# Linear attention and an MLP on one core: three feature buffers, two x buffers, another order of the first loads, longer runs of half-array matmuls, and a last tile in two column parts

## The chip, the cores and the metric

The kernel runs on one core of a Trainium2 chip. The metric is the time on the device in microseconds. A program written with the Tile framework issues to five engines, each with its own queue: PE (TensorE, matmuls), DVE (VectorE), ACT (ScalarE), POOL (GpSimd) and SP (SyncE, which here only issues DMAs). Each queue runs in order; semaphores order the queues among each other.

## The reference

Eight batches, eight heads, 576 tokens, a head width of 64, 128 features. All inputs are float32, the output too.

```python
def phi(x):
    proj = einsum('bhsd,df->bhsf', x, w_phi)
    proj = proj - max(abs(proj), axis=-1, keepdims=True)
    return concatenate([exp(proj), exp(-proj)], axis=-1)
q_p, k_p = phi(q), phi(k)
kv = einsum('bhsf,bhsd->bhfd', k_p, v)
z = sum(k_p, axis=2)
num = einsum('bhsf,bhfd->bhsd', q_p, kv)
den = einsum('bhsf,bhf->bhs', q_p, z)[..., None] + 1e-06
x = (num / den) laid out as [batch, token, head * 64]          # 8 x 576 x 512
xn = (x - mean(x)) / sqrt(var(x) + 1e-06) * g_ln               # over the 512 columns
out = x + maximum(xn @ w_ch1, 0) @ w_ch2                       # 512 -> 2048 -> 512
```

## The kernel before, in words

The work is cut into four pairs of batches. A pair has 2 x 576 = 1152 tokens, which are nine tiles of 128 tokens. Tiles 0 to 7 are the first 512 tokens of the two batches; tile 8 holds the last 64 tokens of both (the "tails", tensors kx, qx, vx).

The attention of a pair is done in eight units; there are 32 units in all, numbered 0 to 31. In pairs 1 to 3 a unit is one head of both batches; in pair 0 it is two heads of one batch. Two units form a group, and a load brings k, q or v of a group (of a unit at the very start). A unit runs through these steps:

- q and k are turned so that the head's 64 columns lie on the partitions (tile qkT). In pair 0 TensorE does it (qkT_ps, line 531, with a copy on VectorE or ScalarE); in later pairs an engine casts to bfloat16 (qkb) and a DMA transposes (line 514).
- pm (line 561): the projections of k and of q, eight matmuls each. They use 64 rows of the array, the half `e` for one of two heads or batches. In the profile they are 64*128, all other matmuls 128*128. One side takes two PSUM banks.
- maxima of |pm| on VectorE (line 581); exp of the maxima (emk, emq, line 597) and exp(pm), exp(-pm) of k (EB, line 612) on ScalarE; GpSimd scales v by the maxima (vv, lines 626 to 635).
- pt and ea (lines 656, 662): the features of q in the other layout. The tails have steps of their own: kx and qx transposed (line 400), px (line 410), their maxima mx (line 424), and the exponentials EBx and eax. emk of a group holds the tails' value in one column, written first.
- kv (lines 681, 686) from EB and vv, copied to KV on ScalarE (line 693); num (line 715) from KV and ea, then numc and rden on VectorE (lines 721 to 733) and the division, which writes x on GpSimd (line 739).

EB, vv and ea have two buffers each, x (nine tiles of a pair) has three, and num is cut into parts so that a PSUM bank is enough.

The MLP of a pair takes three tiles at a time. VectorE makes the mean and variance (line 858), VectorE or GpSimd the centred value times g_ln (xc, lines 866 to 876; this is where the norm vector `gln` is read), transposes give xT (TensorE in pair 0, line 923; DMA later, line 908). hT_ps (line 973, function `first`) is a block of 128 of the 2048 hidden columns for 384 tokens, four matmuls of 384 columns; ScalarE or VectorE applies relu into hT (lines 981, 983; 32 buffers). ch_ps (line 1005, function `second`) sums 16 matmuls of 512 columns for one tile; VectorE adds x (the result, line 1012), and SP issues the store (line 951, or line 956 for tile 8, two DMAs). The MLP of a pair is mixed with the attention of the next.

The order of the work is not the order of the loops. Each step is given to a planner (class `Order`) with an estimated duration, the engines that may take it, the keys that it reads and writes, and the resource that it takes (`"B"`: 8 PSUM banks). `due` walks backwards to give each step a rank; `run` then walks forwards, lets each engine take the waiting step of lowest rank whose resources are free, and writes the instructions out in that order. Keys such as `("EA", e, n % 2)` stand for buffers. So a changed number of buffers, load order or rule in `run` gives each queue a new order. The planner's estimates are no measurements.

SP and ACT issue DMAs that share eight semaphores in turn, so a ninth issue waits until the first has landed.

Of the kernel before, what the change touches and what calls it, by code (L numbers as in the profile page):

```python
# [23 lines left out]
LAG = {"PE": 0.24, "DVE": 0.20, "ACT": 0.23, "POOL": 0.22, "SP": 0.1, "DMA": 1.8, "CAST": 1.8}  # L24

# [8 lines left out]
class Order:  # L34
# [73 lines left out]
    def run(self):  # L108
# [13 lines left out]
        while events:  # L122
            now = events[0][0]
            while events and events[0][0] <= now + 1e-9:
                _, kind, _, op, _ = heapq.heappop(events)
                if kind == 1:
                    for engine in op.alts:
                        key = op.ready if engine in ("DMA", "CAST") else op.rank
                        heapq.heappush(waiting[engine], (key, op.number, op))
                elif kind == 0:  # L130
                    for name, n in op.release or ():
                        room[name] += n
            for engine, queue in waiting.items():
                if free[engine] > now + 1e-9 or not queue:
                    continue
                passed, held, op = [], set(), None
                while queue:
                    item = heapq.heappop(queue)
                    op = item[2]
                    if op.taken:  # L140
                        op = None
                        continue
                    if op.acquire is None or (
                        op.acquire[0] not in held and room[op.acquire[0]] >= op.acquire[1]
                    ):
                        break
                    held.add(op.acquire[0])
                    passed.append(item)
                    op = None
                for item in passed:  # L150
                    heapq.heappush(queue, item)
                if op is None:
                    continue
                op.taken, op.at = True, (now, engine)
                if op.acquire:
                    room[op.acquire[0]] -= op.acquire[1]
                us = op.alts[engine]
                if engine == "DMA" and free.get("CAST", 0.0) > now:
                    shared = free["CAST"] - now
                    us = 4.0 * us if 4.0 * us <= shared else us + shared * 0.75  # L160
                end = now + us
                if engine == "PE" and op.rows != rows:
                    rows = op.rows
                    end += 0.1
                lag = LAG[engine] if op.lag is None else op.lag
                free[engine] = end
                done.append((op, engine))
                heapq.heappush(events, (end, 2, op.number, op, None))
                heapq.heappush(events, (end + lag, 0, op.number, op, None))
                for o in op.users:  # L170
                    same = len(o.alts) == 1 and engine in o.alts
                    o.ready = max(o.ready, end + (0.1 if same else lag))
                    o.left -= 1
                    if not o.left:
                        offer(o)
# [8 lines left out]
def kernel(  # L184
# [21 lines left out]
    NT = 9  # L206
# [6 lines left out]
    NBUF = 3  # L213
    RN = 384
# [5 lines left out]
    NX = 3  # L220
# [21 lines left out]
    ea_bufs = [consts.tile([P, 2, MX * P], BF16, name=f"ea{i}") for i in range(2)]  # L242
# [5 lines left out]
    sched = Order({"B": 8})  # L248
# [37 lines left out]
    def dma(queue, rank, nbytes, dst, src, r=(), w=()):  # L286
# [7 lines left out]
        add(queue, {"SP": 0.55, "ACT": 0.55, "POOL": 0.84}[queue], rank, emit, r=r, w=(key, *w, *chain), lag=0.0)  # L294
        if queue == "POOL":
            add("CAST", 4.2, rank, None, r=(key,), w=w)
        else:
            add("DMA", nbytes / 340.0 / 1000.0, rank, None, r=(key,), w=w)
# [29 lines left out]
    def load_tails(t, pair, batches, queue, rank):  # L328
        key = "kqv"[0 if t is k else 1 if t is q else 2] + "x"
        for half in range(2):  # L330
            ps_ = slice(half * 64, half * 64 + 64)
            if pair == 0 and t is not q:
                (b,) = batches
                slots = range(4 * b, 4 * b + 4)
                off, step = (b * H + half) * S * D, 2 * S * D
            else:
                slots = range(H)
                off, step = (2 * pair + half) * H * S * D, S * D
            sl = slice(slots[0], slots[-1] + 1)
            if t is v:  # L340
                dst = vx_bufs[pair % 2][ps_, sl, half, 0:D]
            else:
                dst = (qx_bufs if t is q else kx_bufs)[pair % 2][ps_, sl, :]
            dma(
                queue, rank, 25000 * len(slots), dst,
                dram(t, off + 512 * D, [[D, 64], [step, len(slots)], [1, D]]),
                w=[(key, half, pair % 2, s) for s in slots],
            )
# [155 lines left out]
    def a_trans(u, V):  # L504
        n, g = u["n"], u["g"]
        pool, tag, res = ps_B, "B", "B"
        if u["pair"]:
# [14 lines left out]
            add("SP", 1.27, V, turn, r=[("qkb", n % 2)], w=[("turn", n), *ks], lag=0.0)  # L522
            add("DMA", 1.0, V, None, r=[("turn", n), ("qkb", n % 2)], w=ks)
# [28 lines left out]
    def a_main(u, V, sides):  # L552
# [14 lines left out]
        for i in sides:  # L567
# [3 lines left out]
                + ([("EB", e, n % 2) for e in range(2)] if i else []),  # L571
# [3 lines left out]
    def a_side(u, i, V):  # L575
# [32 lines left out]
        def exps(e):  # L608
            if "EB" not in u:
                u["EB"] = att.tile([P, 2, MX, F], BF16, tag="EB", name="EB")  # L610
# [10 lines left out]
        def scale_main(t):  # L621
            if t == 1:
                u["vv"] = att.tile([P, 2, NT + 1, D1], BF16, tag="vv", name="vv")
# [17 lines left out]
        for e in range(2):  # L641
            add("ACT", 0.96, V, lambda e=e: exps(e), r=[("pm", 1, n, e), ("m", 1, n % 3, e)],
                w=[("EB", e, n % 2)], release=[("B", 1)])
        vdata = [*main_keys(u, "v"), *tail_keys(u["pair"], u["slot"], "v")]
        add("POOL", 1.5, V, lambda: scale_main(1), r=[("em", 1, n % 3), *vdata],
            w=[("vv", 1, n % 2)])
        add("POOL", 1.5, V, lambda: scale_main(0),
            r=[("en", n % 3), ("vv", 1, n % 2), *vdata], w=[("vv", 0, n % 2)])

    def a_feat(u, V):  # L650
        n = u["n"]

        def products(e):
            u["EA"] = ea_bufs[n % 2]
# [12 lines left out]
        for e in range(2):  # L667
            add("PE", mm(1, 512), V, lambda e=e: products(e), r=["wb", ("qkT", 0, n % NQ)],
                w=[("pt", n, e), ("EA", e, n % 2)], acquire=("B", 1))
            add("ACT", 0.96, V, lambda e=e: exps(e), r=[("pt", n, e)], w=[("EA", e, n % 2)],  # L670
                release=[("B", 1)])

    def a_kv(u, V):
# [17 lines left out]
        def copy():  # L691
# [5 lines left out]
            r=[(what, t, n % 2) for what in ("EB", "vv") for t in range(2)] + [("EBx", g % 2)],  # L697
# [84 lines left out]
    def nums(u, part, V):  # L782
        n, pair = u["n"], u["pair"]
        x = x_bufs[pair % NX]
        keys = [("EA", 0, n % 2), ("EA", 1, n % 2), ("KV", n % NKV)]
# [61 lines left out]
    def x_stats(pr, r, V):  # L847
# [38 lines left out]
        def rstd():  # L886
            sl = slice(ts[0], ts[-1] + 1)
# [7 lines left out]
    def x_trans(pr, r, slot_c, V):  # L895
# [5 lines left out]
        if pr["pair"]:  # L901
            for i in range(n):
# [10 lines left out]
                add("SP", 1.27, V, turn, r=[("xc", slot_c, i)], w=[key, *wk], lag=0.0)  # L913
                add("DMA", 0.5, V, None, r=[key, ("xc", slot_c, i)], w=wk)
# [32 lines left out]
    def store(pr, t, o):  # L947
        b0 = 2 * pr["pair"]
        if t < MX:
            b, j = b0 + t // 4, t % 4  # L950
            nc.sync.dma_start(
                out=dram(out, (b * S + j) * DM, [[4 * DM, P], [1, DM]]), in_=o
# [7 lines left out]
    HB = 2 * JC  # L960

    def moe(pr, V):
# [34 lines left out]
        def second(r, i0, n, V):  # L997
# [3 lines left out]
            def products():  # L1001
                if j0 == 0:
                    ch[t] = ps_B.tile([P, DM], FP32, tag="B", name="ch_ps")
                for jj in range(j0, j0 + n):
                    nc.tensor.matmul(  # L1005
                        ch[t], hT[r, jj][:, rt * P : (rt + 1) * P], w2_sb[:, jj, :],
# [3 lines left out]
            def result():  # L1010
                ch["o", t] = o = out_pool.tile([P, DM], FP32, tag="o", name="o")
                nc.vector.scalar_tensor_tensor(  # L1012
                    out=o, in0=ch[t], scalar=pr["rstd"][:, t : t + 1], in1=x[:, t, :],
                    op0=ALU.mult, op1=ALU.add,
# [3 lines left out]
            add("PE", mm(n, DM), V, products,  # L1018
                r=[("rstd", pair % 2, t)] + [hkey[r, jj] for jj in js]
                + [("w2", jj) for jj in (js if j0 or pair else range(JC))],  # L1020
                w=[("ch", pair, t)], acquire=("B", 1) if j0 == 0 else None)
            if j0 + n == JC:
                ok = ("o", counts["o"] % 3)
                counts["o"] += 1
                add("DVE", 0.67, V - 30.0, result,
                    r=[("ch", pair, t), ("rstd", pair % 2, t)] + [("x", pair % NX, t, h) for h in range(H)], w=[ok], release=[("B", 1)])
                key = ("store", pair, t)
                add("SP", 0.42 if t < MX else 1.2, 0.0, lambda: store(pr, t, ch["o", t]),
                    r=[ok], w=[key], lag=0.0)
                add("DMA", 0.8, 0.0, None, r=[key, ok])  # L1030

        NR = len(tiles)
        for r in range(NR + 1):
# [5 lines left out]
            for jj in range(JC):  # L1039
# [5 lines left out]
                if r > 0:  # L1045
                    i, end = jj * m, (jj + 1) * m
                    while i < end:
                        n = min(end - i, JC - i % JC)
                        ahead[0] = E_S0 if pair == 0 and r <= TILES0 else E_MOE
                        second(r - 1, i, n, V)  # L1050
                        i += n
                    V += MOE_STEP * m / 3
        return V
# [5 lines left out]
    for p_ in range(NPAIR):  # L1059
        sizes = (3, 3, 3) if p_ == 0 else (3, 3, 3)  # L1060
# [4 lines left out]
        })  # L1065
    for n in range(NU):
# [15 lines left out]
    for half in range(2):  # L1082
        dma("ACT", 0.0, 32768, wphi_f[half * D : (half + 1) * D, :], w_phi, w=[("wphi", half)])
    load_main(q, 0, [0], "ACT", 0.1)
    load_tails(k, 0, [0], "SP", 0.2)
    load_main(v, 0, [0], "SP", 0.3)
    load_tails(v, 0, [0], "SP", 0.4)
    dma("ACT", 0.5, 262144, gln_sb, dram(moe_g_ln, 0, [[0, P], [1, DM]]), w=["gln"])
    load_main(k, 0, [1], "SP", 0.6)
    load_main(q, 0, [1], "ACT", 0.6)  # L1090
# [24 lines left out]

    load_main(k, 2, [0, 1], "SP", 3.0)
# [8 lines left out]
    for n in range(NU + 2):  # L1125
        V = start(n)
        step = start(n + 1) - V
        if n < NU:
# [20 lines left out]
            if n == GATE:  # L1149
                kx1 = kx_bufs[1]  # L1150
                add("POOL", 0.1, V, lambda: nc.gpsimd.memset(kx1[:, :, 0:1], 0.0),
                    r=[("vv", 0, n % 2)], w=[k_ for s_ in range(H) for k_ in tail_keys(1, s_, "k")])
            for i_ in WEIGHTS.get(n, ()):
                after = [("vv", 0, n % 2)]
# [87 lines left out]
```

## Time and profile before

The median of 13 runs is 382.99 us (380.49 to 384.79).

| what | value |
|---|---|
| the profiled execution's own time | 383.77 us |
| its span | 382.0 us |
| mean granted TensorE clock | 0.986 |
| first hT_ps matmul | 46.56 us |
| PE idle, 0 to 20 us | 8.4 us |
| PE idle, 20 to 60 us | 7.6 us |
| PE idle, 60 to 120 us | 3.4 us |
| PE idle, 120 to 300 us | 1.4 us |
| unit 1's first pm matmul | 12.06 us |
| GpSimd's first vv | 10.19 us |
| largest groups on PE: hT_ps, ch_ps | 150.4 us and 148.4 us busy |

A page lists busy time by engine, then 40 slices of the span in which each digit is a busy share in tenths, then DMA queues, the chain of work that ended last, and the costliest groups of instructions. A row of the timeline has the start, the time that the merged instructions cover, engine, line, operation, what is written and read, and a count; in square brackets stand the idle time ahead of it and what ended it. PE matmuls are pipelined: each is shown with its latency, so rows of PE overlap, and the distance of two starts is what a matmul costs.

### The profile page before, as it was taken

To read this page: it belongs to the slowest core of one execution; us is meant where nothing else is said; L and a number is where in the kernel's file an instruction comes from. 1 tells how busy PE (TensorE), PEld (TensorE's weight loads), DVE (VectorE), ACT (ScalarE), POOL (GpSimd) and SP (SyncE) were. 2 spreads that over 40 slices of the span, in tenths; PEclk is the share of its full clock that TensorE was granted. 3 is DMA by queue.
4 is the path that set the end of the run, shared out by engine and by line. 5 is a ranking of instruction groups with operands and counts; after the bars stand their busy time and mean duration, and the time that the engine had idled before them with its cause. 6 is when DMAs were issued, how large, how long until landed. Compare 5 with 4: busy or idle time off the path is not lost.

```text
span 382.0 us, 9102 instructions
## 1 busy us (share of the span) xinstructions
PE 356.2 (93%) x3332; PEld 208.7 (55%) x3332; DVE 280.1 (73%) x722; ACT 251.0 (66%) x641; POOL 205.3 (54%) x365
## 2 busy tenths in 40 slices
PE   4787889899999999998999999999999999999994
PEld 1565656546555555654566545655556546555541
DVE  4799998998989979976779889978688785000111
ACT  3899697698959627876789647866688416433310
POOL 4699687646886728944557467944447432000000
PEclk9989799999999999999999999999999999999999
DMA  7999999955968845384739835612200136110112
GB/s 202 332 274 186 177 314 261 223 126 137 255 148 212 213 144 112 71 231 84 221 76 219 205 99 123 154 30 63 78 0 29 43 96 102 30 52 27 55 41 71
DMA packets 88605, 52.70 MB, mean 138 GB/s; under 512 B 55024, under 2 KB 83824, under 8 KB 88560
## 3 DMA queue, kind: packets, MB, share of 16 engines
q1 hardware_dynamic: 83488, 47.07, 48.2%
q0 software_dynamic: 4224, 4.19, 6.9%
q10 hardware_dynamic: 848, 0.85, 0.8%
q8 instruction: 26, 0.43, 0.5%
q14 instruction: 19, 0.16, 0.2%
HBM read 37.03 MB, written 9.44 MB: 122 GB/s over the span
## 4 chain that ended last, share of the span: by engine, by line
PE 74%; DMA 7%; ACT 7%; DVE 5%; POOL 2%; issue 2%; SPq 1%; DVEq 0%; ACTq 0%; POOLq 0%
PE ch_ps L1005 29%; PE hT_ps L973 28%; PE num L715 4%; DMA qkT<-qkb 4%; PE pm L561 4%; PE kv L686 3%; PE pt L656 3%; ACT EB L612 3%; ACT ea L662 2%; DVE m L581 1%; DMA kx<-in_k_dram 1%; DMA qk<-in_k_dram 1%; PE kv L681 1%; DMA qk<-in_q_dram 1%; POOL vv L626 1%
## 5 line engine op out<-in xcount | busy, mean ns | idle before, releaser
L973 PE MATMUL hT_ps<-xT,w 128*128 128x384 bf16 x768 | 150.4, 326 | 1.4 <-ACT ea L662 0.6
L1005 PE MATMUL ch_ps<-w,hT 128*128 128x512 bf16 x576 | 148.4, 379 | 0.6 <-DVE numc L721 0.6
L983 ACT ACTIVATE hT<-hT_ps 128x384 bf16<-128x384 f32 x127 | 61.8, 496 | 64.4 <-PE hT_ps L973 63.8
L973 PEld LDWEIGHTS <-w 128*128 128x128 bf16 x768 | 71.0, 98 | 53.4 <-issue 2.2
L581 DVE TENSOR_REDUCE m<-pm 128x4 f32<-128x512 f32 x128 | 81.2, 677 | 7.4 <-PE pm L561 7.1
L739 POOL TENSOR_TENSOR x<-numc,rden 128x192 bf16<-128x192 f32 (+1 forms) x112 | 51.6, 471 | 59.7 <-DVE rden L733 59.4
L1005 PEld LDWEIGHTS <-hT 128*128 128x128 bf16 x576 | 52.8, 98 | 48.1 <-issue 0.8
L612 ACT ACTIVATE EB<-pm 128x512 bf16<-128x512 f32 x128 | 69.4, 621 | 8.3 <-DVE m L581 8.1
L662 ACT ACTIVATE ea<-pt 128x512 bf16<-128x512 f32 x128 | 67.2, 627 | 6.1 <-PE pt L656 5.8
L1012 DVE SCALAR_TENSOR_TENSOR o<-ch_ps,rstd,x 128x512 f32<-128x512 f32 x36 | 26.5, 742 | 52.8 <-PE ch_ps L1005 41.0
L626 POOL TENSOR_TENSOR vv<-v,emk 128x512 bf16<-128x512 f32 x32 | 33.5, 1048 | 38.8 <-ACT emk L597 26.3
L721 DVE TENSOR_TENSOR numc<-num,emq 128x195 f32<-128x195 f32 (+1 forms) x96 | 32.2, 346 | 14.4 <-PE num L715 11.7
L981 DVE TENSOR_SCALAR hT<-hT_ps 128x384 bf16<-128x384 f32 x65 | 34.5, 539 | 5.6 <-PE hT_ps L973 5.0
L715 PEld LDWEIGHTS <-ea 128*128 128x128 bf16 x512 | 28.6, 100 | 17.0 <-issue 5.1
L715 PE MATMUL num<-KV,ea 128*128 128x65 bf16 x512 | 31.5, 196 | 3.3 <-ACT KV L693 1.6
L626 POOL TENSOR_TENSOR vv<-v,en 128x512 bf16<-128x512 f32 x32 | 34.4, 1075 | 0.0
L727 DVE TENSOR_TENSOR numc<-numc,num 128x195 f32<-128x195 f32 (+1 forms) x100 | 33.3, 343 | 1.0
L561 PEld LDWEIGHTS <-qkT 64*128 64x128 bf16 x512 | 16.1, 98 | 17.4 <-issue 13.4
L858 DVE BATCH_NORM_STATS2 st<-x 128x6 f32<-128x512 bf16 x36 | 24.2, 672 | 1.2 <-POOL x L739 1.2
L686 PE MATMUL kv<-vv,EB 128*128 128x65 bf16 x512 | 24.9, 198 | 0.0
L686 PEld LDWEIGHTS <-EB 128*128 128x128 bf16 x512 | 22.4, 101 | 2.7 <-issue 0.9
L656 PE MATMUL pt<-qkT,wbk 128*128 128x512 bf16 x64 | 23.3, 410 | 0.1
(67 smaller groups left out, 389.5 us busy)
## 6 DMA issues: line engine op xcount, KB each, us to landing
out_dram<-o SPq DMA_DIRECT2D x32, 256.0 KB, 2.5
qk<-in_k_dram SPq DMA_DIRECT2D x28, 256.0 KB, 4.8
v<-in_v_dram SPq DMA_DIRECT2D x28, 256.0 KB, 3.3
qk<-in_q_dram SPq DMA_DIRECT2D x26, 256.0 KB, 5.3
w<-in_moe_w_ch_dram POOLq DMA_DIRECT2D x8, 512.0 KB, 8.6
qk<-in_k_dram SPq DMA_DIRECT2D x2, 512.0 KB, 6.2
qk<-in_q_dram SPq DMA_DIRECT2D x2, 512.0 KB, 6.9
v<-in_v_dram SPq DMA_DIRECT2D x2, 512.0 KB, 7.1
```

Of the source, the lines that this page charges most:

```text
L581: nc.vector.reduce_max(out=u["m", i].rearrange("p (c e) -> p e c", e=2)[:, e], in_=u["pm", i, e], axis=AX.X, apply_absolute_value=True,)
L612: nc.scalar.activation(u["EB"][:, t, e * 4 : (e + 1) * 4].rearrange("p c f -> p (c f)"), u["pm", 1, e].rearrange("p c f -> p (c f)"), AF.E ...
L626: nc.gpsimd.tensor_tensor(out=u["vv"][:, t, 0:MX, 0:D], in0=vb[:, uu, :].rearrange("p (c d) -> p c d", d=D), in1=bcast(e[:, 0:MX], 2, D), ...
L656: nc.tensor.matmul(u["pt", e], wbk[:, e, :], u["qkT"][:, 0:512], start=True, stop=True)
L662: nc.scalar.activation(u["EA"][:, t, e * 512 : (e + 1) * 512], u["pt", e], AF.Exp, scale=(1.0, -1.0)[t],)
L686: nc.tensor.matmul(ps[:, t, c // 4, :], EB[:, t, (c % 2) * 4 + c // 2, :], vv[:, t, c, :], start=False, stop=(t == 0 and c == MX - 1), ski ...
L715: nc.tensor.matmul(ps[:, t, i, :], lhsT, rhs, start=(j == 0), stop=(j == len(terms) - 1))
L739: nc.gpsimd.tensor_tensor(out=dst, in0=st["numc"][:, i : i + cnt, 0:D], in1=bcast(st["rden"][:, i : i + cnt], 2, D), op=ALU.mult,)
L973: nc.tensor.matmul(st["ps"][:, 0:cols], w1_sb[:, kc, jj * P : (jj + 1) * P], pr["xT", r][:, kc, 0:cols], start=(kc == 0), stop=(kc == KC - 1),
L981: nc.vector.tensor_relu(h_sb[:, 0:cols], st["ps"][:, 0:cols])
L983: nc.scalar.activation(h_sb[:, 0:cols], st["ps"][:, 0:cols], AF.Relu)
L1005: nc.tensor.matmul(ch[t], hT[r, jj][:, rt * P : (rt + 1) * P], w2_sb[:, jj, :], start=(jj == 0), stop=(jj == JC - 1),)
```

## The change

- Buffers: ea, EB and vv have three (`NE`), x has two (`NX`), hT has 28 (`HB`).
- `run`: after a half-array step (`rows`, the pm products) PE takes another such step that is ready, if its PSUM banks are free and its rank is less than `STAY` = 10 behind the first in the queue.
- A resource `"S"` of eight stands for the DMA semaphores in the plan: each SP and ACT issue takes one, its transfer gives it back.
- The first loads: one half of w_phi is issued by SP, k and q of unit 1 come ahead of v of unit 0 and of the tails, and the norm vector is loaded by SP after the groups of units 2 and 3 instead of by ACT among the first.
- The last pair's last three tiles are taken in the order 8, 6, 7; tile 7 is finished in two column parts, 384 and 128 wide, each with its own PSUM tile, result and store. The last step of the loop is emitted after the loop, four matmuls at a time.
- `load_tails` is written differently, with the same loads.

```diff
+STAY = 10.0
...
-                while queue:
+                if engine == "PE" and rows:
+                    near = sorted(i for i in queue if i[2].rows and not i[2].taken)
+                    near = [i for i in near if room[i[2].acquire[0]] >= i[2].acquire[1]]
+                    if near and near[0][0] < queue[0][0] + STAY:
+                        op = near[0][2]
+                while queue and op is None:
...
+    NE = 3
...
-    NX = 3
+    NX = 2
...
-    ea_bufs = [consts.tile([P, 2, MX * P], BF16, name=f"ea{i}") for i in range(2)]
+    ea_bufs = [consts.tile([P, 2, MX * P], BF16, name=f"ea{i}") for i in range(NE)]
...
-    sched = Order({"B": 8})
+    sched = Order({"B": 8, "S": 8})
...
-        add(queue, {"SP": 0.55, "ACT": 0.55, "POOL": 0.84}[queue], rank, emit, r=r, w=(key, *w, *chain), lag=0.0)
+        add(queue, {"SP": 0.55, "ACT": 0.55, "POOL": 0.84}[queue], rank, emit, r=r, w=(key, *w, *chain), lag=0.0,
+            acquire=None if queue == "POOL" else ("S", 1))
...
-            add("DMA", nbytes / 340.0 / 1000.0, rank, None, r=(key,), w=w)
+            add("DMA", nbytes / 340.0 / 1000.0, rank, None, r=(key,), w=w, release=[("S", 1)])
...
-                u["EB"] = att.tile([P, 2, MX, F], BF16, tag="EB", name="EB")
+                u["EB"] = att.tile([P, 2, MX, F], BF16, tag="EB", name="EB", bufs=NE)
...
-                u["vv"] = att.tile([P, 2, NT + 1, D1], BF16, tag="vv", name="vv")
+                u["vv"] = att.tile([P, 2, NT + 1, D1], BF16, tag="vv", name="vv", bufs=NE)
...
-    HB = 2 * JC
+    HB = 28
...
-        def second(r, i0, n, V):
+        def second(r, i0, n, V, c0=0, c1=DM):
...
-                        ch[t], hT[r, jj][:, rt * P : (rt + 1) * P], w2_sb[:, jj, :],
+                        ch[t, c0], hT[r, jj][:, rt * P : (rt + 1) * P], w2_sb[:, jj, c0:c1],
...
+        LAST = (len(tiles[-1]) - 1) * JC
...
+                        if pair == NPAIR - 1 and r == NR and i >= LAST:
+                            break
                         second(r - 1, i, n, V)
...
+        if pair == NPAIR - 1:
+            for c0, c1 in ((0, 384), (384, DM)):
+                for jj in range(0, JC, 4):
+                    second(NR - 1, LAST + jj, 4, V, c0, c1)
+                    V += 1.0
...
+    pairs[-1]["tiles"][-1] = [MX, MX - 2, MX - 1]
...
     load_main(k, 0, [0], "SP", 0.0)
-    for half in range(2):
-        dma("ACT", 0.0, 32768, wphi_f[half * D : (half + 1) * D, :], w_phi, w=[("wphi", half)])
+    for e_, queue in enumerate(("ACT", "SP")):
+        dma(queue, 0.0, 32768, wphi_f[e_ * D : (e_ + 1) * D, :], w_phi, w=[("wphi", e_)])
     load_main(q, 0, [0], "ACT", 0.1)
-    load_tails(k, 0, [0], "SP", 0.2)
+    load_main(k, 0, [1], "SP", 0.2)
+    load_main(q, 0, [1], "ACT", 0.2)
     load_main(v, 0, [0], "SP", 0.3)
-    load_tails(v, 0, [0], "SP", 0.4)
-    dma("ACT", 0.5, 262144, gln_sb, dram(moe_g_ln, 0, [[0, P], [1, DM]]), w=["gln"])
-    load_main(k, 0, [1], "SP", 0.6)
-    load_main(q, 0, [1], "ACT", 0.6)
+    load_tails(k, 0, [0], "SP", 0.4)
+    load_tails(v, 0, [0], "SP", 0.5)
     load_main(v, 0, [1], "SP", 0.7)
...
+    dma("SP", 3.0, 262144, gln_sb, dram(moe_g_ln, 0, [[0, P], [1, DM]]), w=["gln"])
     load_main(k, 2, [0, 1], "SP", 3.0)
```

## The prediction

> **What bounds the kernel now.** I read the page's totals first, then its forty slices, then stages of the span, and last the instructions around one suspected cost.
>
> ```profile
> PE 356.2 (93%) x3332; PEld 208.7 (55%) x3332; DVE 280.1 (73%) x722; ACT 251.0 (66%) x641; POOL 205.3 (54%) x365
> ...
> PE   4787889899999999998999999999999999999994
> ```
>
> TensorE is busy almost everywhere except in the first six slices and the last. The view by stage says how much is left to win (columns: stretch, length, busy time of PE, PEld, DVE, ACT, POOL with counts, clock, DMA share, GB/s):
>
> ```profile
> 20.00:46.50 26.50, 20.69 (x290) 15.31 (x289) 25.81 (x79) 23.21 (x64) 23.82 (x50) 0.82 1.07 207
> ...
> 60.00:120.00 60.00, 56.63 (x609) 33.76 (x605) 54.03 (x142) 48.00 (x128) 41.81 (x74) 1.00 0.81 186
> 120.00:300.00 180.00, 178.58 (x1745) 104.49 (x1744) 150.05 (x382) 128.17 (x327) 108.85 (x182) 1.00 0.48 123
> ```
>
> From 120 us on PE is idle for 1.4 us in 180; nothing there gets shorter unless PE itself does less. From 20 us to 46.5 us (the first hT_ps group starts at 46.56) VectorE is busy for 25.8 of 26.5 us, and ScalarE and GpSimd nearly as long: that stage is limited by the three elementwise engines, and it begins when their first inputs arrive. So the change can gain in three places: an earlier start, less PE work, a shorter end.
>
> **Part 1, fewer changes between half-array and full-array matmuls.** The pm products use 64 rows of the array (64*128), everything else 128. Around one pm block the timeline of PE reads:
>
> ```profile
> 192.97 0.81 PE L973 MATMUL hT_ps<-xT,w 128*128 128x384 bf16 x4
> 193.72 0.40 PE L561 MATMUL pm<-wbk,qkT 64*128 64x128 bf16 x8
> 194.05 0.82 PE L1005 MATMUL ch_ps<-w,hT 128*128 128x512 bf16 x3
> ```
>
> Groups of four hT_ps matmuls that follow each other start 0.65 us apart, so pm could start at 192.97 + 0.65 = 193.62; it starts at 193.72, 0.10 late. It then holds PE for 0.33 us. Where two blocks stand together, the second adds 0.23 only:
>
> ```profile
> 184.90 0.40 PE L561 MATMUL pm<-wbk,qkT 64*128 64x128 bf16 x8
> 185.13 0.39 PE L561 MATMUL pm<-wbq,qkT 64*128 64x128 bf16 x8
> 185.45 0.82 PE L1005 MATMUL ch_ps<-w,hT 128*128 128x512 bf16 x3
> ```
>
> So leaving costs 0.33 - 0.23 = 0.10 us too: 0.10 per change of mode. PE shows no idle time for it; it hides in "busy". I counted the changes in the order written out for each kernel: 106 before, 76 after. Ahead of the first hT_ps they rise from 26 to 30, where PE waits for others anyway. Behind it they fall from 80 to 46: 34 x 0.10 = 3.4 us; I take **-3.2 us**, since PE was busy for only 11.7 of the 13.5 us from 46.5 to 60. The Trainium skill ("TensorEngine Tiling (Array Packing)", Key Properties) says a change of mode drains the array, without a price; "TensorE: Matmul & The Clock Gate" (Single matmul latency) puts the constant part of a lone warm matmul at 166 ns. Priced as a whole lone latency, the estimate would be 34 x 0.166 = 5.6 us. The trace has the thing itself at 0.10, so 3.2 stands and 5.6 is the far end. The near end is 2.2: the same 34 with a third of it spent waiting for other engines.
>
> The price of staying: a pm pair takes two PSUM banks of the eight earlier than before, k and q together four. They come free after four maxima (0.68 us each) on VectorE and four exponentials (0.62) on ScalarE, about 2.7 us. Other groups then have four banks, and one hT_ps group of four and three ch_ps matmuls, which open about one new bank, pass per 1.3 us. In the pair at 184.90 above nothing waited. I cost it at 0; without that cover it is the rival below.
>
> **Part 2, the first loads.** The DMA queue of SP before:
>
> ```profile
> 0.74 0.45 SPq L291 DMA_DIRECT2D qk<-in_k_dram  x1
> 1.25 1.41 SPq L291 DMA_DIRECT2D kx<-in_k_dram  x2
> 2.70 0.72 SPq L291 DMA_DIRECT2D v<-in_v_dram  x1
> 3.56 1.26 SPq L291 DMA_DIRECT2D vx<-in_v_dram  x2
> 6.49 0.37 SPq L291 DMA_DIRECT2D qk<-in_k_dram  x1
> ```
>
> The k of unit 1 is issued at 6.49 only, held by the kx transfer, and on PE the consequence is
>
> ```profile
> 6.61 0.37 PE L400 MATMUL xT_ps<-ident,kx 128*128 128x128 bf16 x2 [1.10 <-DMA kx<-in_k_dram]
> ...
> 10.51 1.03 PE L531 MATMUL qkT_ps<-ident,qk 128*128 128x128 bf16 x8 [0.93 <-DMA qk<-in_k_dram]
> 12.06 0.61 PE L561 MATMUL pm<-wbk,qkT 64*128 64x128 bf16 x8 [0.52 <-DVE qkT L282]
> ```
>
> After, SP issues k0, one half of w_phi, k1, v0, kx (two), vx (two), v1. Five issues of some 0.5 us put k1 at about 1.8 us. kx loses: its second half is queued behind a wait for k0 (landed at 3.52), so it is issued until about 4.3. From issue to landing kx took 3.9 us here, and the 64 KB loads of k tails have a median of 5.7: it lands at **8.2 to 10.0** against 6.5. The skill speaks against the reordering ("DMA: Bandwidth & Descriptors", Issuing engines are not separate DMA queues): all queues share the same 16 DMA engines, so an earlier k1 and v0 are paid for by kx. By that rule alone 2 x 256 KB at the 225 GB/s of the slice from 4 to 8 us put kx at 6.5 + 2.3 = 8.8, within my bracket; the DMA share there is 0.85, so the rule counts.
>
> What waits for kx: in the new PE order the kx transposes stand behind unit 0's pt and ahead of unit 1's pm. Unit 0's pm itself no longer waits for kx: limited by ScalarE's copies of qkT (5.55 + 2 x 0.58), it starts near 6.5 instead of 6.92. Unit 1's pm starts about 1.0 us behind kx's landing (transpose, copy, px), at 9.2 to 11.0 instead of 12.06: 1.1 to 2.9 us earlier. GpSimd gets its first emk later: behind px stand about 3.2 us of ScalarE work (two EB, two ea, two EBx), so vv starts at 12 to 14 instead of 10.19. Against that, GpSimd stood idle for 1.9 us before unit 1's vv (15.10) and 1.5 us at 19.67, idle times that disappear when both units are ready together, as the three vv buffers allow. So GpSimd lies between 1.6 us ahead and 0.2 us behind at 20 us; VectorE, idle for 2.7 us between 8 and 24 us, gains up to 3. I take **-2.0 us** at the first hT_ps, with bounds of +1.5 (kx past its bracket, GpSimd late) and -4 (all of VectorE's idle time, and some of the 3.4 us that PE idles from 60 to 120). The half of w_phi leaves ScalarE's queue (0.5 us, while it waits for TensorE).
>
> The norm vector's load (256 KB) moves from ScalarE's queue to SP's, behind unit 2's and 3's loads and ahead of unit 4's: one issue of 0.5 us and 1 us of transfer, which delay loads that are used 10 us later. Its first reader, xc, runs at 38.98. Cost 0.
>
> **Part 3, buffers.** Three ea, EB and vv decouple the engines; with VectorE busy for 25.8 of 26.5 us that adds nothing beyond part 2. x falls from three buffers to two, so unit 16's and unit 24's first x waits for the last result of pair 0 and pair 1. In the new order 16 hT_ps, 8 pm and 18 kv matmuls, some 3.6 us, lie between pair 1's last ch_ps and that point, against a result of 0.74 us; pair 0 has 8.6 us. Cost 0; without that cover, at most 1 us each. hT falls from 32 to 28 buffers: the 13th hT of a group reuses the first of the group before, read a step (1.3 us) earlier. Cost 0.
>
> **Part 4, the end.** Before:
>
> ```profile
> 376.32 1.41 DVE L1012 SCALAR_TENSOR_TENSOR o<-ch_ps,rstd,x 128x512 f32<-128x512 f32 x2 [5.06 <-PE ch_ps L1005]
> 377.76 1.11 SPq L956 DMA_DIRECT2D out_dram<-o  x2
> ```
>
> PE ends at 376.93, the result at 377.73 (+0.80), the last store is issued at 378.3 (+1.37). After, a full tile's result starts half a microsecond before PE's end (the last eight matmuls are 128 wide, 8 x 0.055); it ends at +0.35, the narrow result (130 columns on VectorE took 0.28) at +0.65. One full and one narrow store issue of 0.36 put the last issue at +0.73: 0.6 us earlier. Sixteen matmuls of 512 columns become 16 of 384 and 16 of 128: at 0.162 + 0.055 against 0.216 almost nothing, at most 0.1. **-0.5 us**, bounds 0 and -1.2.
>
> **Sum.** -3.2 - 2.0 + 0 - 0.5 = -5.7. The profiled execution took 383.77 (span 382.0), so it would take 378.1; the median, 382.99, is 0.8 below it, which gives **377.3**.
>
> **Rivals.** (a) The early start is lost: kx at 10 us or later makes GpSimd late by what the others gain. ScalarE, VectorE and GpSimd, full together from 20 us, speak for it, GpSimd's idle 3.4 us against it. Then 383.0 - 3.2 - 0.5 = 379.3. (b) More is gained: the stalls up to 120 us go too, and the start brings 4: 375.0. (c) Slower: staying in the half-array mode takes PSUM banks before their turn, and PE waits for a free bank once in each of the 24 units of pairs 1 to 3. The wait decides from 5.7 / 24 = 0.24 us a unit; at 0.36, half of one maximum, it costs 8.6, which ends at 386. Against it: pm pairs already stand together without an idle gap. (d) The change does nothing measurable: the stays cost about what they save (0.24 us a unit), 383.
>
> **How the numbers follow.** The forecast 0.52, (a) 0.20, (b) 0.08, (c) 0.14, (d) 0.06. A measurement of this kernel tells about 0.5% (1.9 us) from no change. Faster: 0.52 + 0.20 + 0.08, less 0.02 for the edge of (a): 0.78; same 0.07; slower 0.15. The forecast's own range is 375.5 to 379.2. To leave out 2 in 10, mostly (c), the range runs from 373.5 (switches at 166 ns, start at -4) to 383.5.
>
> **What would show it.** Part 1: fewer entries of pm blocks, pm in runs of 16, PE's idle time from 120 to 300 us still under 3 us; (c) would put new PE waits there, released by VectorE or ScalarE. Part 2: unit 1's pm at 9 to 11 us, vv's first start at 12 to 14, the first hT_ps near 44.5. Part 4: from PE's end to the span's end 4.5 us instead of 5.1. The prediction is wrong if the first hT_ps comes no earlier, or if PE waits grow behind 60 us.

## The result and the profile after

The changed kernel takes 378.96 us (median of 11 runs, 376.92 to 381.53) against 383.19 us for the kernel before (48 runs). The ratio is 0.9897, with a 95% interval from 0.9867 to 0.9927: faster by 1.0%, about 4 us. Ratios leave out executions that took over 1.5% longer than the fastest of the same kernel. The forecast was 377.3 and rival (a) 379.3; the direction and the range were right, and of the 5.7 us expected some 4 came.

The page of the profiled execution (378.96 us, span 377.2 us), first the totals, then PE's forty slices:

```profile
PE 351.7 (93%) x3348; PEld 208.7 (55%) x3348; DVE 280.1 (74%) x726; ACT 251.0 (67%) x638; POOL 208.4 (55%) x367
...
PE   3877699799999999999999999999999999999995
```

PE is busy for 4.5 us less with 16 matmuls more, and the first to fifth and the eighth slice still aren't full. The view by stage of the changed kernel, with the columns that the prediction explained:

```profile
20.00:46.50 26.50, 17.98 (x291) 13.87 (x288) 25.69 (x80) 24.03 (x68) 24.91 (x49) 0.91 1.03 210
46.50:60.00 13.50, 12.83 (x153) 8.45 (x152) 13.04 (x40) 12.37 (x34) 12.78 (x28) 0.92 1.09 249
60.00:120.00 60.00, 57.05 (x621) 34.70 (x618) 56.17 (x144) 48.79 (x129) 43.41 (x77) 1.00 1.08 219
120.00:300.00 180.00, 178.56 (x1759) 105.76 (x1758) 150.25 (x391) 128.41 (x325) 106.95 (x180) 1.00 0.46 116
```

The stage up to 46.5 us is as full on VectorE, ScalarE and GpSimd as before, and it did not become shorter. The first hT_ps matmul, on PE's timeline:

```profile
47.44 1.46 PE L985 MATMUL hT_ps<-xT,w 128*128 128x384 bf16 x4
```

It was at 46.56. From there to PE's last matmul the kernel before needed 376.93 - 46.56 = 330.4 us, the changed one 372.91 - 47.44 = 325.5. PE's idle time explains 1.5 us of these 4.9: from 46.5 to 60 us it fell from 1.76 to 0.67, from 60 to 120 us from 3.37 to 2.95, and behind 120 us it is 1.42 and 1.44. The other 3.4 is work that PE does in less time: 34 changes of mode at 0.10, if the price in the prediction holds. A higher granted clock is not behind it: from 46.5 to 60 us the changed kernel had 0.92 and the kernel before 0.98, from 60 to 300 us both had 1.00. So the two profiled spans differ by +0.9 (start) - 1.5 (waits) - 3.4 (modes) - 0.8 (end) = -4.8 us. This is bookkeeping over one execution of each kernel; the medians and the ratio say 4.2 and 4.0.

### The profile page after: what moved, and what is told of

Read it like the earlier page. It is cut to its first block, busy times and chain, and to the rows that moved or that the text cites. A ratio compares the mean times of both kernels' runs of the same rounds, so it can differ in the third digit from the quotient of the medians.

```text
span 377.2 us, 9121 instructions
## 1 busy us (share of the span) xinstructions
PE 351.7 (93%) x3348; PEld 208.7 (55%) x3348; DVE 280.1 (74%) x726; ACT 251.0 (67%) x638; POOL 208.4 (55%) x367
## 4 chain that ended last, share of the span: by engine, by line
PE 74%; ACT 8%; DMA 8%; DVE 6%; issue 1%; POOL 1%; SPq 0%; DVEq 0%; POOLq 0%
PE hT_ps L985 29%; PE ch_ps L1017 28%; DMA qkT<-qkb 6%; PE num L726 4%; PE pm L572 3%; PE kv L697 3%; ACT EB L623 3%; ACT ea L673 3%; PE pt L667 3%; DVE m L592 1%; DMA qk<-in_q_dram 1%; DMA qk<-in_k_dram 1%; DVE xc L877 1%; PE kv L692 1%; PE px L420 1%
## 5 line engine op out<-in xcount | busy, mean ns | idle before, releaser
L1017 PE MATMUL ch_ps<-w,hT 128*128 128x512 bf16 (+2 forms) x592 | 148.1, 373 | 0.2 <-DVE mv L870 0.2
L592 DVE TENSOR_REDUCE m<-pm 128x4 f32<-128x512 f32 x128 | 80.2, 676 | 8.1 <-PE pm L572 7.9
L1017 PEld LDWEIGHTS <-hT 128*128 128x128 bf16 x592 | 53.8, 98 | 47.6 <-issue 1.2
L750 POOL TENSOR_TENSOR x<-numc,rden 128x192 bf16<-128x192 f32 (+1 forms) x112 | 51.8, 476 | 46.0 <-DVE rden L744 44.5
L623 ACT ACTIVATE EB<-pm 128x512 bf16<-128x512 f32 x128 | 70.3, 636 | 9.0 <-DVE m L592 8.8
L673 ACT ACTIVATE ea<-pt 128x512 bf16<-128x512 f32 x128 | 68.3, 647 | 2.8 <-PE pt L667 2.7
L1025 DVE SCALAR_TENSOR_TENSOR o<-ch_ps,rstd,x 128x512 f32<-128x512 f32 (+2 forms) x37 | 26.7, 729 | 52.7 <-PE ch_ps L1017 40.7
L993 DVE TENSOR_SCALAR hT<-hT_ps 128x384 bf16<-128x384 f32 x66 | 35.6, 547 | 6.4 <-PE hT_ps L985 5.8
L883 POOL TENSOR_TENSOR xd<-x,mv 128x512 f32<-128x512 bf16 x17 | 18.3, 1079 | 14.7 <-DVE mv L870 12.9
L697 PE MATMUL kv<-vv,EB 128*128 128x65 bf16 x512 | 24.0, 196 | 0.0
```

Of the source, the lines that this page charges most:

```text
L592: nc.vector.reduce_max(out=u["m", i].rearrange("p (c e) -> p e c", e=2)[:, e], in_=u["pm", i, e], axis=AX.X, apply_absolute_value=True,)
L623: nc.scalar.activation(u["EB"][:, t, e * 4 : (e + 1) * 4].rearrange("p c f -> p (c f)"), u["pm", 1, e].rearrange("p c f -> p (c f)"), AF.E ...
L673: nc.scalar.activation(u["EA"][:, t, e * 512 : (e + 1) * 512], u["pt", e], AF.Exp, scale=(1.0, -1.0)[t],)
L697: nc.tensor.matmul(ps[:, t, c // 4, :], EB[:, t, (c % 2) * 4 + c // 2, :], vv[:, t, c, :], start=False, stop=(t == 0 and c == MX - 1), ski ...
L750: nc.gpsimd.tensor_tensor(out=dst, in0=st["numc"][:, i : i + cnt, 0:D], in1=bcast(st["rden"][:, i : i + cnt], 2, D), op=ALU.mult,)
L993: nc.vector.tensor_relu(h_sb[:, 0:cols], st["ps"][:, 0:cols])
```

## What happened in the first 20 us

SP's queue, then PE's, in the changed kernel (timeline):

```profile
1.88 0.58 SPq L300 DMA_DIRECT2D qk<-in_k_dram  x1
...
3.01 1.33 SPq L300 DMA_DIRECT2D kx<-in_k_dram  x2
```
```profile
6.02 0.61 PE L542 MATMUL qkT_ps<-ident,qk 128*128 128x128 bf16 x4 [1.83 <-DMA qk<-in_q_dram]
7.31 0.61 PE L572 MATMUL pm<-wbk,qkT 64*128 64x128 bf16 x8 [0.68 <-ACT qkT L289]
...
9.33 1.06 PE L667 MATMUL pt<-qkT,wbk 128*128 128x512 bf16 x2
10.18 0.31 PE L410 MATMUL xT_ps<-ident,kx 128*128 128x128 bf16 x1
...
11.18 0.61 PE L572 MATMUL pm<-wbk,qkT 64*128 64x128 bf16 x8
```

k of unit 1 is issued at 1.88 us instead of 6.49, and its first pm (the last row) starts at 11.18 instead of 12.06. But q of unit 0 lands at 6.02; in the kernel before it was there at 4.90:

```profile
4.90 0.61 PE L531 MATMUL qkT_ps<-ident,qk 128*128 128x128 bf16 x4 [0.77 <-DMA qk<-in_q_dram]
```

Both q loads were issued at nearly the same time (1.38 and 1.36 us, on ScalarE's queue). What moved beside them is in the view by stage, from 2 to 4 and from 4 to 6 us (the last two columns are DMA share and GB/s), for the kernel before and the changed one:

```profile
2.00:4.00 2.00, 0.47 (x4) 0.35 (x4) 0.20 (x2) 0.02 (x1) 1.89 (x5) 1.00 0.95 286
4.00:6.00 2.00, 0.75 (x6) 0.34 (x4) 0.62 (x3) 0.45 (x1) 1.44 (x4) 1.00 0.68 183
```
```profile
2.00:4.00 2.00, 0.41 (x4) 0.34 (x4) 0.20 (x2) 0.02 (x1) 1.89 (x5) 1.00 0.68 202
4.00:6.00 2.00, 0.19 (x2) 0.00 (x0) 1.50 (x4) 0.00 (x0) 1.44 (x4) 1.00 1.01 326
```

From 2 us to q's landing the kernel before moved 2 x 286 + 0.9 x 183 = 737 KB, the changed one 2 x 202 + 2 x 326 = 1056 KB: some 320 KB more passed through the same engines ahead of q's last byte, about 1 us at either rate (286 or 326 GB/s). Besides, the changed kernel moved 168 KB less from 2 to 4 us; why is open. The delay is not that of one execution: in the six kernels here that take the new loads, q's transposes start at 5.69 to 6.54 us, in the six with the old order or one close to it at 4.85 to 5.46. Which of the moved loads does it (k and q of unit 1, v of unit 0) isn't separated.

So unit 0's pm starts at 7.31, later than the 6.92 before, and kx is turned at 10.18 instead of 6.61. That isn't kx's own landing: its two halves were issued at 3.01 and 3.70 and took 5.5 and 5.0 us, so both were there by 8.7, and the row at 10.18 shows no wait. Ahead of it in PE's queue stands unit 0's pt (9.33), and that stands behind the late q. GpSimd's first vv, behind px, starts at 13.58 instead of 10.19. Unit 1's pm gained 0.9 us, unit 0's lost 0.4, and GpSimd lost 3.4 us. Even the gain is not sure: in `x_nostay` and `x_oldtail` below, which have the same loads and buffers, unit 1's pm starts at 12.03 and 12.02, and vv at 14.54 and 14.42.

The time of the first hT_ps holds more than the loads. PE's granted clock (third number from the end) just before and behind it, in the kernel before and in the changed one:

```profile
44.00:48.00 4.00, 3.80 (x36) 2.40 (x35) 3.89 (x15) 2.45 (x7) 1.50 (x4) 0.62 1.14 214
```
```profile
44.00:48.00 4.00, 4.00 (x42) 2.64 (x40) 3.66 (x12) 3.08 (x9) 3.99 (x7) 0.50 0.94 254
```

In the changed kernel PE is busy for all of these 4 us, at half the clock. `x_mix` below, granted 1.00 in this stretch, has the earliest first hT_ps of all, at 45.65. How much of the changed kernel's 0.9 us is the clock's, no run separates.

## The experiments

The ratios are to the kernel before on the same chip (medians 382.4 to 383.3 us). "Changes" are changes between half-array and full-array matmuls in the order written out, in all and ahead of the first hT_ps; the kernel before has 106 and 26, the changed one 76 and 30.

**The rule that stays, alone and left out.** `x_bstay` is the kernel before with nothing but the rule in `run`; `x_nostay` is the changed kernel with the rule switched off.

```diff
# x_bstay, on the kernel before
+                if engine == "PE" and rows:
...
+                    if near and near[0][0] < queue[0][0] + STAY:
+                        op = near[0][2]
-                while queue:
+                while queue and op is None:
# x_nostay, on the changed kernel
-STAY = 10.0
+STAY = -1e9
```

> The kernel before with that rule alone. Changes of mode 78 instead of 106 (54 instead of 80 behind the first hT_ps). Theory: 2.6 us faster than before (ratio 0.993). Rival: same as before, with PE waits for banks in place of the changes.

> The changed kernel without the rule that keeps PE in the half-array mode; all else as changed. Changes of mode 102 instead of 76 (72 instead of 46 behind the first hT_ps). Theory (0.10 us per change, PE-bound): 26 x 0.10 = 2.6 us slower than the changed kernel, so about 1.3 us faster than before (ratio 0.996), PE's end late by as much and its idle time from 120 to 300 us unchanged. Rival (the stays are free of gain, since they take banks early): within 0.5 us of the changed kernel.

`x_bstay` has 78 and 24 changes and takes 380.28 us: 0.9924 (0.9892 to 0.9955), or 2.9 us (1.7 to 4.1) for 26 fewer behind the first hT_ps, 0.11 us each. `x_nostay` has 102 and 30 and takes 383.06 us, 0.9997 (0.9968 to 1.0026; the expected 0.996 lies just below): 1.0% or 3.8 us above the changed kernel for 26 more, 0.15 each. The two intervals together leave 2.2 to 5.4 us, 0.09 to 0.21 each. By PE's end in the two profiles it is 375.18 - 372.91 = 2.3 us, 0.09 each; that profile belongs to the fastest of the twelve runs of `x_nostay`, so the timed number weighs more. The rule is the larger part of the whole gain, and without it the rest of the change brings nothing that can be measured.

A new order can also change what PE waits for, so the time alone doesn't give the price of a change of mode. PE's work from the first hT_ps to its last matmul, that stretch less its idle time, is nearer to it: 323.8 us before and 321.5 in `x_bstay`, 320.4 in the changed kernel and 322.3 in `x_nostay`. That is 2.3 and 1.9 us for 26 changes, 0.09 and 0.07 each. In `x_bstay` the other part of the shorter profiled span is idle time, 1.5 us less behind the first hT_ps, which itself comes 0.6 us later.

On `x_bstay` the price of staying would show as PE waiting for banks behind 120 us. The waits of PE from 120 to 300 us are (what waited, for what, us in total, times, longest):

```profile
PE hT_ps L981 <- DVE o L1020: 0.6, 1, 0.6
```

One wait in 180 us, in 24 units: rival (c) needed 0.24 us in each. In the changed kernel itself the same view has two waits, of 0.8 us for VectorE and 0.5 for ScalarE, in an idle time that did not grow (1.44 us).

**The loads, undone and alone.** `x_oldloads` is the changed kernel with the first loads of before; `x_bloads` is the kernel before with the new first loads and nothing else.

```diff
# x_oldloads, on the changed kernel (x_bloads is the reverse, on the kernel before)
-    for e_, queue in enumerate(("ACT", "SP")):
-        dma(queue, 0.0, 32768, wphi_f[e_ * D : (e_ + 1) * D, :], w_phi, w=[("wphi", e_)])
+    for half in range(2):
+        dma("ACT", 0.0, 32768, wphi_f[half * D : (half + 1) * D, :], w_phi, w=[("wphi", half)])
-    load_main(k, 0, [1], "SP", 0.2)
-    load_main(q, 0, [1], "ACT", 0.2)
+    load_tails(k, 0, [0], "SP", 0.2)
     load_main(v, 0, [0], "SP", 0.3)
-    load_tails(k, 0, [0], "SP", 0.4)
-    load_tails(v, 0, [0], "SP", 0.5)
+    load_tails(v, 0, [0], "SP", 0.4)
+    dma("ACT", 0.5, 262144, gln_sb, dram(moe_g_ln, 0, [[0, P], [1, DM]]), w=["gln"])
+    load_main(k, 0, [1], "SP", 0.6)
+    load_main(q, 0, [1], "ACT", 0.6)
...
-    dma("SP", 3.0, 262144, gln_sb, dram(moe_g_ln, 0, [[0, P], [1, DM]]), w=["gln"])
```

> The changed kernel with the first loads in the order of before (w_phi and the norm vector too). Theory now, after the changed kernel's first hT_ps came at 47.4 instead of 46.6 us: the new order delays unit 0's q by 1.1 us and kx by 3 us, and that eats what the earlier k of unit 1 gives; then the old order is equal or up to 1.5 us faster than the changed kernel, with the first pm at 6.9 and the first hT_ps at 46 us. Theory of the prediction (the new order gains 2 us): 2 us slower than the changed kernel.

> The kernel before with the new order of the first loads alone. Theory now: no gain, 0 to 1.5 us slower than before (ratio 1.000 to 1.004), unit 0's q at about 6.0 us. Theory of the prediction: 2 us faster (0.995).

`x_oldloads` takes 377.38 us: 0.9859 (0.9817 to 0.99). That is not slower than the changed kernel, whose interval it overlaps. Its unit 0 has q at 4.85 and kx at 6.81, its unit 1 starts pm at 11.81, and its first hT_ps stands at 46.56 us, 0.9 earlier than with the new loads. So the new order of loads didn't bring the start forward at all. The other kernels with three buffers agree, one execution each: 47.56 and 48.30 us with the new loads (`x_nostay`, `x_oldtail`), 45.65 and 47.16 with other orders (`x_mix`, `x_oldfirst`, below). `x_oldtail` starts like the changed kernel, so 0.9 us is also what one execution may differ from another here.

`x_bloads` takes 391.43 us, 1.0235 (1.0189 to 1.028): the new loads alone cost 8 to 9 us, far more than either expectation. PE's timeline in it:

```profile
22.34 0.61 PE L531 MATMUL qkT_ps<-ident,qk 128*128 128x128 bf16 x4 [4.46 <-DMA qk<-in_k_dram]
22.74 0.32 PE L681 MATMUL kv<-vv,EBx 128*128 128x130 bf16 x1
...
53.01 0.29 PE L681 MATMUL kv<-vv,EBx 128*128 128x130 bf16 x1 [2.32 <-DVE numc L727]
...
57.24 1.35 PE L973 MATMUL hT_ps<-xT,w 128*128 128x384 bf16 x4
```

PE stands still for 4.46 us at four transposes that wait for a load of k. In the order written out they belong to unit 4, whose k is issued at 13.25 us only (512 KB, two units), and directly behind them stands the first kv of unit 0. In the kernel before that kv runs at 14.94. Ahead of it this kernel has 36 transposes of k and q, the kernel before 24, the changed kernel 32 and none of unit 4. GpSimd then has nothing to divide:

```profile
27.57 0.51 POOL L739 TENSOR_TENSOR x<-numc,rden 128x192 bf16<-128x192 f32 x1 [6.54 <-PE num L715]
```

The first kv comes 7.8 us late: GpSimd's vv, which it reads, had already come 4.8 us late (15.01 against 10.19), and the wait of 4.46 us stands ahead of it. The first hT_ps comes 10.7 us late (57.24 against 46.56), of which some 2 are made up later; a second wait of 2.32 us, for numc of VectorE, stands shortly ahead of it. How the 10.7 divide among these was not isolated.

**What mends it: the plan's resource S, or the buffers.** `x_bloads_s` adds S to `x_bloads`. `x_ne2nx3` is the changed kernel with two ea, EB and vv, and three x.

```diff
# x_bloads_s, on x_bloads
-    sched = Order({"B": 8})
+    sched = Order({"B": 8, "S": 8})
# and acquire=("S", 1) at each SP and ACT issue, release=[("S", 1)] at its transfer
# x_ne2nx3, on the changed kernel
-    NE = 3
+    NE = 2
...
-    NX = 2
+    NX = 3
```

> The kernel before with the new order of loads and with the DMA semaphores as a resource in the plan. In the new loads alone PE stood for 4.5 us at transposes of a k that had not landed, ahead of unit 0's kv. Theory (the plan trusted loads that the chip delivers later): the resource mends it, 383 to 385 us. Rival (two buffers are the reason): 389 to 392 as without the resource.

> The changed kernel with two ea, EB and vv and three x, as before the change; new loads, stays, tail and the DMA resource kept. Theory (the third buffers are what lets the plan live with the new order of loads: the kernel before with that order was 9 us slower): 4 to 9 us slower than the changed kernel, the first hT_ps at 52 us or later. Theory of the prediction (the buffers add nothing beyond an earlier start): within 1 us of the changed kernel.

`x_bloads_s` takes 387.34 us, 1.0139 (1.0091 to 1.0188): S takes back 4 us, less than expected, and the same transposes still wait, for 3.53 us; its first hT_ps comes at 55.80. `x_ne2nx3` takes 385.95 us, 1.01 (1.0065 to 1.0136), slower than the kernel before though it has the rule, S and the new tail. Its timeline of PE:

```profile
19.95 0.40 PE L542 MATMUL qkT_ps<-ident,qk 128*128 128x128 bf16 x4 [2.32 <-DMA qk<-in_k_dram]
20.19 0.22 PE L692 MATMUL kv<-vv,EBx 128*128 128x130 bf16 x1
...
54.23 1.42 PE L985 MATMUL hT_ps<-xT,w 128*128 128x384 bf16 x4
```

Again 36 transposes stand ahead of the first kv, four of them unit 4's. From 20 to 46.5 us each of its three elementwise engines is less busy than in any other kernel with the rule:

```profile
20.00:46.50 26.50, 21.30 (x280) 15.93 (x280) 21.80 (x71) 22.93 (x62) 21.30 (x47) 0.74 0.93 188
```

VectorE is busy for 21.80 us there, against 25.69 in the changed kernel. Of its 4.7 us of idle time one piece of 2.05 (at 21.34) stands right behind the wait for k; the rest are gaps of up to 0.6 us, and later the wait for numc is there again (2.27 us at 49.99). So the worth of the buffers is measured, but that the one late k is all of its cause isn't shown: the wait is half of that in `x_bloads`, and the first hT_ps is still 7.7 us later than before.

**Two buffers with the old loads.** `x_oldloads_ne2` is `x_oldloads` with `NE = 2` and `NX = 3`.

> The changed kernel with the first loads of before and the buffers of before (two ea, EB and vv, three x): the other half of the crossing of loads and buffers. Measured so far: new loads with three buffers 0.9897, new loads with two 1.0100, old loads with three 0.9859. Theory (the third buffers are needed only by the new order of loads): within 1 us of old loads with three, about 378. Rival (the buffers gain by themselves): 380 or more.

As expected for the case that only the new loads need the buffers, it takes 378.14 us, 0.9889 (0.9837 to 0.9941), with 24 transposes ahead of the first kv and the first hT_ps at 46.0 us. With it the two edits form a square; the rule, S and the new tail are in all four:

| ratio to the kernel before (95%) | old loads | new loads |
|---|---|---|
| two ea, EB, vv; three x | 0.9889 (0.9837 to 0.9941) | 1.0100 (1.0065 to 1.0136) |
| three ea, EB, vv; two x | 0.9859 (0.9817 to 0.9900) | 0.9897 (0.9867 to 0.9927) |

With the old loads the third buffers change nothing that the intervals can tell. With the new loads they are worth 2.0%, 7.8 us. Read the other way: the new loads cost 2.1% where there are two buffers, and nothing that can be told where there are three. Neither edit earns anything that shows in the time; the buffers pay for the loads.

**Mixtures of the load orders.** `x_mix` takes the old order with k of unit 1 ahead of v of unit 0 and the norm vector late; `x_oldfirst` takes the old order, and leaves only the norm vector late.

```diff
# the first loads of x_mix, on x_oldloads
     load_tails(k, 0, [0], "SP", 0.2)
+    load_main(k, 0, [1], "SP", 0.25)
     load_main(v, 0, [0], "SP", 0.3)
...
-    dma("ACT", 0.5, 262144, gln_sb, dram(moe_g_ln, 0, [[0, P], [1, DM]]), w=["gln"])
-    load_main(k, 0, [1], "SP", 0.6)
...
+    dma("SP", 3.0, 262144, gln_sb, dram(moe_g_ln, 0, [[0, P], [1, DM]]), w=["gln"])
# x_oldfirst: the move of gln alone
```

> The changed kernel with another order of the first loads: as before the change (unit 0's q ahead of the second half of w_phi, k tails second on SP), but with unit 1's k ahead of unit 0's v, and the norm vector late. Theory (unit 0's q and kx must not be delayed; the norm vector's 256 KB can leave): q at 4.9 us, kx at 6.5, unit 1's k at 6 to 7 us instead of 10.5, and 1.5 to 3 us faster than the changed kernel (376 to 377.5). Rival (the elementwise engines limit the stage whatever comes first): equal to the changed kernel with all old loads, 377.4.

> The changed kernel with the first loads of before, but the norm vector late as in the change. Theory (the late norm vector is the good part of the new order): unit 1's k no later than 10 us, and 0.5 us faster than with all old loads, about 377. Rival (it neither helps nor harms): equal, 377.4.

`x_mix` takes 378.45 us, 0.9901 (0.9865 to 0.9937). Its start looks the best of all (unit 1's pm at 10.67, the first hT_ps at 45.6 us), yet its time can't be told from that of the changed kernel, and the gain of 1.5 to 3 us that was expected isn't there. `x_oldfirst` takes 380.42 us with a wide spread (eight executions, 377.13 to 382.51; two slower ones are left out), 0.9924 (0.9882 to 0.9966). That misses what was expected of it, overlaps the others, and settles nothing. No version was shown to beat the changed kernel; `x_oldloads` has the lowest ratio.

**The old tail.** `x_oldtail` keeps everything but the last tile's two parts and the order 8, 6, 7.

```diff
-                        if pair == NPAIR - 1 and r == NR and i >= LAST:
+                        if False:
...
-        if pair == NPAIR - 1:
+        if False:
...
-    pairs[-1]["tiles"][-1] = [MX, MX - 2, MX - 1]
```

> The changed kernel with the last pair's tiles in the old order 6, 7, 8 and the last tile whole. Theory: 0.5 to 0.8 us slower than the changed kernel; from PE's end to the span's end 5.1 us instead of 4.3. Rival (the tail is hidden): same as changed.

It takes 379.86 us, 0.9938 (0.9908 to 0.9968): 0.4% more than the changed kernel, with intervals that overlap, so the time doesn't settle it. The profile shows the piece itself. SP's last store rows, in `x_oldtail` and then in the changed kernel:

```profile
373.71 1.11 SPq L968 DMA_DIRECT2D out_dram<-o  x2
```
```profile
371.47 1.11 SPq L968 DMA_DIRECT2D out_dram<-o  x2
373.28 0.81 SPq L962 DMA_DIRECT2D out_dram<-o  x2
```

PE ends at 372.89 in `x_oldtail` and at 372.91 in the changed kernel. The two issues of tile 8 (1.11 us) now come before PE's end, and what follows it are the two stores of tile 7 (0.81 us). From PE's end to the span's end it is 377.8 - 372.89 = 4.9 us with the old tail and 377.2 - 372.91 = 4.3 with the new one.

## Why the prediction was right in sign and nearly 2 us off

**Part 1 (-3.2) held.** Alone the rule gave 2.9 us for 26 changes, which at 0.10 are 2.6; leaving it out cost 2.3 us by profile and 3.8 by time. The 0.10 us read off two rows of PE lies inside the 0.07 to 0.15 of these runs (work, PE's end and time). The 0.166 us that the prediction took from the Trainium skill's page "TensorE: Matmul & The Clock Gate" (Single matmul latency) for its far end is above all of them, though the interval of `x_nostay` by time reaches 0.21. In the changed kernel two and three pm blocks stand together without a gap:

```profile
190.47 0.81 PE L1017 MATMUL ch_ps<-w,hT 128*128 128x512 bf16 x3
191.21 0.40 PE L572 MATMUL pm<-wbq,qkT 64*128 64x128 bf16 x8
191.44 0.39 PE L572 MATMUL pm<-wbk,qkT 64*128 64x128 bf16 x8
191.66 0.39 PE L572 MATMUL pm<-wbq,qkT 64*128 64x128 bf16 x8
191.98 0.82 PE L985 MATMUL hT_ps<-xT,w 128*128 128x384 bf16 x4
```

Leaving the mode after the third block still takes 0.32 against 0.22 us between blocks: the same 0.10.

**Part 2 (-2.0) is the step that failed.** The working let kx alone pay for the earlier k1 and v0, and kept unit 0's q at its old time; from there came a first pm "near 6.5" (by its own sum, 5.55 + 2 x 0.58, it is 6.7). Measured: q 1.1 us later (6.02) and the first pm at 7.31. kx itself landed by 8.7, inside its bracket and near the 8.8 worked out from the rule, but PE turned it only at 10.18, behind the pt that the late q had held up. So unit 1's pm came at 11.18, just behind its bracket of 9.2 to 11.0, and at 12.0 in the two other executions with these loads and three buffers. The first vv at 13.58 is in its bracket of 12 to 14; the 14.42 and 14.54 of those two are not. The first hT_ps was to come near 44.5 us and came at 47.44. The rule that was weighed there, that all queues share the same 16 DMA engines (the Trainium skill, "DMA: Bandwidth & Descriptors", Issuing engines are not separate DMA queues), was applied to kx and not to q, which was in flight on ScalarE's queue when k of unit 1 was put beside it. Nor did the working have a term for the granted clock at the first hT_ps, 0.50 where PE was full. Against `x_oldloads` the term is +0.9 us at the first hT_ps, and by the time between nothing and a loss of 1.5. By its number this is rival (a), whose 379.3 us is 0.3 above the measured median; its reason, a landing of kx at 10 us or later, is not what happened.

**Part 3 (0) was right as a sum and wrong as a reason.** "Adds nothing beyond part 2" took buffers and loads as separate terms. With the old loads the third buffers are indeed worth nothing that the time shows; with the new ones they hold off 7.8 us. Had the change come without them, it would have been slower than before. The forecast had no term for this, because the trace of before has no late load in front of a ready kv.

**Part 4 (-0.5) held:** 4.3 us behind PE's end instead of 5.1 before, and 4.9 with the old tail. Two slips of the working elsewhere change nothing: xc first runs at 38.89 us, not 38.98, and switches at 166 ns with a start at -4 give 372.9, not 373.5.

**Rival (c)** falls with the waits shown above; **(b)** and **(d)** fall with the time. The prediction's sign "wrong if the first hT_ps comes no earlier" did come. By the profiles the start missed its term by 2.9 us (+0.9 for -2.0), and half of that was made good by 1.5 us of shorter waits from 46.5 to 120 us, which no term foresaw. That the total came out inside the forecast's range is in part luck. The profiles point to the third buffers for these waits, one execution each: PE's waits from 46.5 to 120 us that are told by name come to 1.3 us in `x_oldloads` and to 3.7 in `x_oldloads_ne2`, where only the buffers differ. The time doesn't settle it. Within that stretch one wait even grew: the changed kernel's PE waits 1.50 us for xc at 69.17 us, where `x_oldloads` waits 0.33 us.

**Still open.** Why the plan puts unit 4's transposes ahead of unit 0's kv with two buffers and not with three was read off the orders, not traced to a rule of the planner. What S is worth with three buffers was not tried, nor 28 instead of 32 hT buffers by themselves. The counts of x and of ea, EB and vv were only moved together. Whether the old loads are truly better than the new ones in the changed kernel (0.4%) stays within the intervals.

## What to carry to other kernels

Where PE is full, count what its matmuls cost beside their columns: a change of array mode showed no idle time and cost some 0.1 us, and the rule that makes them fewer was worth two thirds or more of this gain by the timed runs (2.9 and 3.8 of 4.0 us). Before moving a load forward, list every load in flight at that moment, on any queue, and move each one's landing in the sum. And where a planner writes the order, cost a load order and the buffers behind it as one edit: look in the new order for a matmul that waits for a late load and stands ahead of ready work.

## What the runs showed that was not expected

- With one wait of 4.46 us for a load in PE's queue the first MLP matmul came 10.7 us later: kv, num and the division stand behind it, and GpSimd was idle for 6.54 us in one piece. With half that wait (2.32 us, `x_ne2nx3`) it still came 7.7 us later.
- k of unit 1 (256 KB), issued by SP at 1.88 us instead of 6.49, and q of unit 1, at 2.0 instead of 2.5, came with unit 0's q landing 1.1 us later, though that q had been issued half a microsecond before them.
- An earlier first hT_ps is not an earlier end: `x_mix` starts its MLP 1.8 us ahead of the changed kernel, and the measured times are the same within their intervals.
